# A convolution by transforms: emptying the transform's bank pairs with two engines, and four smaller moves at its start

## The chip, the cores and the metric

The kernel runs on one core of one Trainium2 chip. The core has TensorE for matmuls (PE in the profile, with its weight loads as PEld), VectorE (DVE), ScalarE (ACT), GpSimd (POOL) and SyncE (SP), which here only issues DMAs. Matmul results go to PSUM, eight banks of 512 fp32 values in each of 128 partitions; ScalarE and VectorE read them from there. The metric is the device time in microseconds (us) of one execution; lower is better. A result is the median of several executions.

## The reference

The reference is a convolution over the sequence with three taps, a batch norm and a SiLU. The input x has 2 images of 2048 rows and 1024 channels, w has 3 taps of 1024 x 1024, all in bf16:

```python
xp = jnp.pad(x, ((0, 0), (P, P), (0, 0)))          # P = K // 2 = 1
y = sum(jnp.einsum('bsc,cd->bsd', xp[:, k:k + S, :], w[k]) for k in range(K))
inv_std = 1.0 / jnp.sqrt(var + 1e-5)
y = (y - mean) * (g * inv_std) + b
return _silu(y)
```

## The kernel before

**The algorithm.** Six neighbouring output rows are computed from eight input rows by way of eight points (0, 1, -1, 2, -2, 1/2, -1/2 and infinity, numbered j = 0 to 7). Input and weights are each transformed to the eight points, multiplied there, and the eight products are combined to six outputs. So 342 groups of six rows (342 columns) need 8 products where a direct convolution would need 18.

**Transform of the input.** The rows come in windows of 128 rows, each with 21 groups of six. For an image `bi` and a channel tile `ct` (128 of the 1024 channels), 16 windows lie in one SBUF tile, 512 KB, called x00 to x07 and x10 to x17 below (image, channel tile). A matmul takes a window as its weights and the constant matrix `rm` (8 points x 21 groups, 168 columns) as what is streamed, so a window costs one matmul of 168 columns (line 231). A job (`Jobs.do`) is 6, 6 or 4 windows, three jobs to a tile, 48 in all. Its results lie in a pair of neighbouring PSUM banks, half of the windows in each, and one instruction of ScalarE ("a", line 249) or VectorE ("d", line 251) empties both banks, 1008 or 672 elements a partition, into `T_sb`, as bf16. The few groups left over in each image are the short tile (`load_small`, `do_short`, line 240).

**Transform of the weights.** The output channels come in 8 tiles of 128 (`dc`). For each, the six inner points need u = e +- o, with e one of w0 + w2, w0 + 4 w2, 4 w0 + w2 and o one of w1, 2 w1, 2 w1. Points 0 and infinity use the raw taps w0 and w2. For dc = 0 POOL makes everything (`prepare_first`): e0, 4 w2, e1, 4 w0, e2, 2 w1, then the six u in the order of points 1, 3, 2, 4, 5, 6. POOL then goes on with dc = 1 (`prepare_second`).

**Products.** A unit is one `dc` and one image. For a point it accumulates eight matmuls of 342 columns, one for each channel tile, into a bank (line 279; in the first unit line 398). ScalarE and VectorE combine the banks (line 294), ScalarE applies SiLU (line 298), SP stores. Units alternate between banks 0 to 3 and 4 to 7. The second unit begins with point 1 of image 1, in bank 7, and needs all of image 1's transform.

**The first unit.** `First` (dc 0, image 0) runs among the transform. Its matmuls are a list `todo`: first points 0 and infinity, channel tile by channel tile, into banks 0 and 1, then points 1, 3, 2, 4, 5 and 6. When a point's eight matmuls are out, its bank is copied, by the engine that `COPIES` names.

**What sets the order.** Each engine works through its own queue in the written order; waits between queues are semaphores. The string `ORDER` gives the order of the start: "Aa" is a job into bank pair A, emptied by ScalarE, a number so many matmuls of the first unit, "s2d" the short tile into bank 2, "z5" five matmuls on zeros, "+" a combination of the first unit put off till there. Pair A is banks 4 and 5, B 6 and 7, C 2 and 3, D 0 and 1. SP issues the loads in the written order (lines 522 to 537): image 0's tiles, among them taps 0 and 2 of the first weights, tap 1, image 1's first tile, its short tile in three pieces, its other tiles, the weights of dc = 1. Six x tiles have buffers, so that a load waits for the matmuls of the tile six before it.

Of the kernel before, what the change touches and what calls it, by code (L numbers as in the profile page):

```python
# [9 lines left out]
FP32 = mybir.dt.float32  # L10
BF16 = mybir.dt.bfloat16
ENG = mybir.EngineType

P = 128
R = 6
NJ = 8
WT = 21
XBUFS = 6
LROWS = 48
SROW = 66  # L20
# [6 lines left out]

BANKS = {"A": 4, "B": 6, "C": 2, "D": 0}
ORDER = (
    "Aa Ba Cd Da Ad Ba s2d z5 Da Bd Ca Da Bd Aa Cd Da Aa Bd Da Cd Aa Bd 3 Ca 2 Aa Bd 2 Ca 2 Aa 2 Bd "  # L30
    "Ca 5 Aa Cd Ba 7 s4d Ca Bd 2 Aa 2 Ca 2 Bd Aa 2 Ca 2 Ad Ba 2 Ca 2 Bd Aa 2 Ca 2 + Ad Ba 2 Ca 2 + 2 "
    "Ba 1 Aa"
)
COPIES = {0: "d", 7: "a", 1: "d", 3: "d", 2: "d", 5: "a"}

@with_exitstack
def kernel(
# [9 lines left out]
    nc = tc.nc  # L47
# [30 lines left out]
    nc.scalar.dma_start(out=rm, in_=rm_in)  # L78
    prm = consts.tile([P, 4, DC], BF16, name="prm")

    zeros = consts.tile([P, 256], FP32, name="zeros")
    nc.vector.memset(zeros, 0.0)
    for _ in range(3):
        nc.tensor.matmul(ps[:, 3, 0:256], lhsT=zeros[:, 0:P], rhs=zeros, start=True, stop=True)
    dummy = consts.tile([P, 2], FP32, name="dummy")
    nc.vector.memset(dummy, 0.0)

# [3 lines left out]
    small = xlpool.tile([P, CT * P], BF16, name="xl")  # L91
    nc.vector.memset(small, 0.0)

    def load_small(bi, cuts=()):
        cuts = (0, *cuts, LROWS)
        for lo, hi in zip(cuts, cuts[1:]):
            nc.sync.dma_start(out=small[bi * SROW + lo:bi * SROW + hi], in_=xl[bi, lo:hi])

    def load_x(bi, ct, parts=1, second=nc.scalar):
        t = xpool.tile([P, NF, P], BF16, name="xw")  # L100
        xt[bi, ct] = t
        step = NF // parts
        for q in range(parts):
            s = slice(q * step, (q + 1) * step)
            (second if q else nc.sync).dma_start(out=t[:, s], in_=x[bi, ct, :, s])
# [18 lines left out]
    def scaled(src, by, eng):  # L124
        t = spool.tile([P, CT, P], BF16, name="w1x2")
        if eng is nc.scalar:
            nc.scalar.mul(t, src, by)
        else:
            eng.tensor_scalar(t, src, by, 0.0, op0=ALU.mult, op1=ALU.add)
        return t  # L130

    def double_w(dc, eng):
        double[dc] = scaled(raw[dc][:, 1], 2.0, eng)

    def even(dc, q, a, b):
        sums[dc, q] = epool.tile([P, CT, P], FP32, name=f"e{q}")
        nc.gpsimd.tensor_tensor(sums[dc, q], a, b, op=ALU.add)  # L137
# [7 lines left out]
    def transform_w(dc, q, signs=(0, 1)):  # L145
        o = double[dc] if q else raw[dc][:, 1]
        if (dc, q) not in wts:
            wts[dc, q] = upool.tile([P, 2, CT, P], BF16, name=f"u{q}")
        for i in signs:
            nc.gpsimd.tensor_tensor(wts[dc, q][:, i], sums[dc, q], o, op=(ALU.add, ALU.subtract)[i])  # L150
# [13 lines left out]
        act_work.append(lambda: double_w(dc, nc.scalar))  # L164
        dve_work.extend((second, third))

    def prepare_first(dc):

        w0, w2 = raw[dc][:, 0], raw[dc][:, 2]

        def evens():
            even(dc, 0, w0, w2)
            even(dc, 1, scaled(w2, 4.0, nc.gpsimd), w0)
            even(dc, 2, scaled(w0, 4.0, nc.gpsimd), w2)

        def left():
            double_w(dc, nc.gpsimd)
            for q, i in ((0, 0), (1, 0), (0, 1), (1, 1), (2, 0), (2, 1)):
                transform_w(dc, q, (i,))

        return evens, left

    def prepare_second(dc):
        w0, w2 = raw[dc][:, 0], raw[dc][:, 2]
# [34 lines left out]
    class Jobs:  # L219
# [6 lines left out]
        def do(self, bank, eng):  # L226
            bi, ct, f, nf = self.todo.pop(0)
            per = nf // 2
            src = ps[:, bank:bank + 2, 0:per * NJ * WT].rearrange("p b (f j n) -> p b f j n", f=per, j=NJ)
            for q in range(nf):  # L230
                nc.tensor.matmul(src[:, q // per, q % per], lhsT=xt[bi, ct][:, f + q], rhs=rm, start=True, stop=True)  # L231
            dst = T_sb[bi][:, ct, :, f * WT:(f + nf) * WT].rearrange("p j (b f n) -> p j b f n", b=2, f=per)
            self.out(dst, src.rearrange("p b f j n -> p j b f n"), eng)

        def do_short(self, bank, eng):
            bi = self.short.pop(0)
# [136 lines left out]
    class First(Unit):  # L373
# [3 lines left out]
        def __init__(self, dc, bi):  # L377
            super().__init__(dc, bi, 0)
            self.sd = dpool.tile([P, 4, NB], FP32, name="sd")
            self.t = [  # L380
                consts.tile([P, 2, NB], FP32, name="f0"), ypool2.tile([P, 2, NB], FP32, name="t1"),
                consts.tile([P, 2, NB], FP32, name="f2"),
            ]
            self.kept = consts.tile([P, 2, NB], FP32, name="kept")
            self.todo = [(j, q, False, ct) for ct in range(CT) for j, q in ((0, 0), (NJ - 1, 1))] + [
                (j, q, add, ct) for j, q, add in (
                    (1, 1, False), (3, 0, False), (2, 1, True), (4, 0, True), (5, 2, False), (6, 2, True),
                ) for ct in range(CT)
            ]
            self.p, self.later = {}, []  # L390

        def do(self):
            j, q, add, ct = self.todo.pop(0)
            if j == 0 or j == NJ - 1:
                lhsT = raw[self.dc][:, 0 if j == 0 else 2, ct]
            else:
                lhsT = wts[self.dc, (j - 1) // 2][:, (j - 1) % 2, ct]
            nc.tensor.matmul(  # L398
                self.bank[q], lhsT=lhsT, rhs=T_sb[self.bi][:, ct, j, :],
                start=not add and ct == 0, stop=ct == CT - 1, skip_group_check=True,  # L400
            )
            if ct == CT - 1:
                self.behind(j, q)
# [28 lines left out]

        def finish(self):
            while self.todo:
                self.do()
            b2, b3 = self.bank[2:]
            self.combine(b3, b2, -0.5, self.p[5])
            for t, a in zip(self.t, (-1.6, -0.4, -0.1)):
                self.combine(t, self.high, a, t)
# [91 lines left out]
            load_w(0, (0, 2))  # L531
    load_w(0, (1,))
    load_x(1, 0, 2, nc.sync)
    load_small(1, (15, 41))
    for ct in range(1, CT):
        load_x(1, ct)
    load_w(1, (0, 1, 2))

    evens, left = prepare_first(0)
    evens()
    left()
    second = list(prepare_second(1))
    second.pop(0)()
    jobs, unit = Jobs(), First(0, 0)
    for token in ORDER.split():
        if token == "+":
            unit.later.pop(0)()
        elif token[0] == "z":  # L550
            z = zeros.bitcast(BF16)
            for _ in range(int(token[1:])):
                nc.tensor.matmul(ps[:, 0, 0:192], lhsT=z[:, 0:P], rhs=z[:, 0:192], start=True, stop=True)
        elif token[0] == "s":
            jobs.do_short(int(token[1]), token[2])
        elif token[0] in BANKS:
            jobs.do(BANKS[token[0]], token[1])
        else:
            for _ in range(int(token)):
                unit.do()  # L560
    for f in unit.later:
        f()
    while unit.todo[0][0] != 6:
        unit.do()
    second.pop(0)()
    seq = [(dc, bi) for dc in range(DC) for bi in range(B)]
    prev = unit
# [105 lines left out]
```

## Time and profile before

| | |
|---|---|
| median of 3 runs | 181.75 us (181.49 to 181.86) |
| the profiled execution | 181.6 us, its span 179.8 us |
| TensorE busy | 173.3 us, 96% of the span |
| VectorE, ScalarE, POOL busy | 148.2, 110.8, 140.6 us |
| x00's first transform matmul | 3.95 us |
| x03's first transform matmul | 10.83 us |
| last transform matmul's job begins | 33.55 us |
| second unit's first matmul | 35.01 us |
| one transform matmul in the queue | 0.073 us |
| one product matmul in the queue | 0.145 us |

Times inside the execution are counted from the start of the span. A matmul's own row shows 0.24 or 0.30 us, because matmuls overlap; what one costs TensorE is the distance between the starts of two. A row of a group gives the number of instructions, their busy time, the mean time of one in ns, and the idle time of the engine ahead of them with what ended it.

### The profile page before, as it was taken

To read this page: it belongs to the slowest core of one execution; us is meant where nothing else is said; L and a number is where in the kernel's file an instruction comes from. 1 tells how busy PE (TensorE), PEld (TensorE's weight loads), DVE (VectorE), ACT (ScalarE), POOL (GpSimd) and SP (SyncE) were. 2 spreads that over 40 slices of the span, in tenths; PEclk is the share of its full clock that TensorE was granted. 3 is DMA by queue.
4 is the path that set the end of the run, shared out by engine and by line. 5 is a ranking of instruction groups with operands and counts; after the bars stand their busy time and mean duration, and the time that the engine had idled before them with its cause. 6 is when DMAs were issued, how large, how long until landed. Compare 5 with 4: busy or idle time off the path is not lost.

```text
span 179.8 us, 3491 instructions
## 1 busy us (share of the span) xinstructions
PE 173.3 (96%) x1372; PEld 124.4 (69%) x1372; DVE 148.2 (82%) x193; ACT 110.8 (62%) x175; POOL 140.6 (78%) x77
## 2 busy tenths in 40 slices
PE   7889999999999999999999999999999999999991
PEld 5768888766666666666666666666666666668891
DVE  1568788987969999998898989898998997766792
ACT  3779989968364747365545654555456454573774
POOL 2499999999997979999999999999979978000000
PEclk9999999999999999999999999999999999999999
DMA  5999993170325030823073306430303020213033
GB/s 161 373 415 380 401 417 132 51 303 4 131 79 231 0 131 0 225 86 131 0 177 133 131 0 127 183 131 2 128 7 131 0 112 25 87 44 128 8 142 121
DMA packets 7507, 24.58 MB, mean 137 GB/s; under 512 B 1123, under 2 KB 1635, under 8 KB 7491
## 3 DMA queue, kind: packets, MB, share of 16 engines
q1 hardware_dynamic: 6915, 23.74, 36.1%
q10 hardware_dynamic: 576, 0.63, 1.0%
q8 instruction: 10, 0.16, 0.4%
q14 instruction: 6, 0.05, 0.1%
HBM read 14.93 MB, written 9.44 MB: 136 GB/s over the span
## 4 chain that ended last, share of the span: by engine, by line
PE 88%; DMA 5%; DVE 3%; ACT 1%; issue 0%; ACTq 0%; DVEq 0%
PE ps L279 75%; PE ps L231 8%; DMA xw<-in_x_dram 5%; PE ps L398 5%; DVE ps L294 2%; DVE t L294 1%; ACT yh L298 1%; ACT T_sb L249 1%; ACTq L78 0%; DVEq L662 0%; DVE sd L294 0%; PE ps L240 0%; PE ps L596 0%; DVEq L294 0%
## 5 line engine op out<-in xcount | busy, mean ns | idle before, releaser
L279 PE MATMUL ps<-T_sb,u 128*128 128x342 bf16 (+2 forms) x768 | 109.4, 298 | 0.0
L279 PEld LDWEIGHTS <-u 128*128 128x128 bf16 x768 | 72.2, 97 | 32.8 <-POOL u L150 0.3
L150 POOL TENSOR_TENSOR u<-e,w1x 128x1024 bf16<-128x1024 f32 x32 | 71.5, 2259 | 5.6 <-DVE e L143 5.5
L279 PE MATMUL ps<-T_sb,wch 128*128 128x342 bf16 (+2 forms) x256 | 39.5, 299 | 0.4 <-DVE ps L294 0.4
L294 DVE SCALAR_TENSOR_TENSOR t<-ps,sd 128x684 f32<-128x684 f32 (+2 forms) x49 | 37.6, 819 | 0.6
L298 ACT ACTIVATE yT<-ps,beta,scale 128x342 bf16<-128x342 f32 (+1 forms) x42 | 29.1, 727 | 12.6 <-PE ps L279 12.6
L150 POOL TENSOR_TENSOR u<-e,wch 128x1024 bf16<-128x1024 f32 x16 | 35.7, 2247 | 0.5
L279 PEld LDWEIGHTS <-wch 128*128 128x128 bf16 x256 | 24.2, 97 | 11.1 <-issue 0.5
L288 ACT COPY pc<-ps 128x342 f32<-128x342 f32 (+2 forms) x32 | 13.6, 424 | 28.4 <-PE ps L279 25.7
L249 ACT CAST T_sb<-ps 128x1008 bf16<-128x1008 f32 (+1 forms) x32 | 27.3, 879 | 3.9 <-PE ps L231 3.5
L251 DVE CAST T_sb<-ps 128x1008 bf16<-128x1008 f32 (+2 forms) x18 | 19.3, 1094 | 9.7 <-PE ps L231 9.2
L294 DVE SCALAR_TENSOR_TENSOR ps<-ps,t 128x684 f32<-128x684 f32 (+2 forms) x32 | 26.5, 829 | 0.7
L294 DVE SCALAR_TENSOR_TENSOR ps<-ps,pc 128x342 f32<-128x342 f32 (+2 forms) x34 | 16.9, 497 | 12.1 <-PE ps L279 8.8
L231 PE MATMUL ps<-rm,xw 128*128 128x168 bf16 x256 | 23.4, 239 | 1.6 <-DMA xw<-in_x_dram 1.4
L143 DVE SCALAR_TENSOR_TENSOR e<-wch 128x1024 f32<-128x1024 bf16 x12 | 24.6, 2052 | 0.0
L231 PEld LDWEIGHTS <-xw 128*128 128x128 bf16 x256 | 19.9, 99 | 4.8 <-DMA xw<-in_x_dram 2.4
L137 POOL TENSOR_TENSOR e<-wch 128x1024 f32<-128x1024 bf16 x8 | 19.0, 2372 | 0.1
L298 ACT ACTIVATE yT<-t,beta,scale 128x684 bf16<-128x684 f32 x15 | 14.4, 958 | 0.0
L294 DVE SCALAR_TENSOR_TENSOR t<-ps,t 128x684 f32<-128x684 f32 (+2 forms) x17 | 13.9, 817 | 0.0
L288 ACT COPY sd<-ps 128x342 f32<-128x342 f32 (+2 forms) x16 | 6.8, 426 | 10.3 <-PE ps L279 9.3
L290 ACT ACTIVATE pc<-ps 128x342 f32<-128x342 f32 (+2 forms) x16 | 7.0, 438 | 8.8 <-PE ps L279 6.1
L294 DVE SCALAR_TENSOR_TENSOR sd<-pc,ps 128x342 f32<-128x342 f32 (+2 forms) x17 | 8.2, 484 | 4.1 <-ACT sd L288 4.0
(45 smaller groups left out, 67.3 us busy)
## 6 DMA issues: line engine op xcount, KB each, us to landing
out_dram<-yT SPq DMA_DIRECT2D x15, 576.0 KB, 2.8
xw<-in_x_dram SPq DMA_DIRECT2D x13, 512.0 KB, 6.4
wch<-in_w_dram SPq DMA_DIRECT2D x7, 768.0 KB, 5.5
xw<-in_x_dram SPq DMA_DIRECT2D x4, 256.0 KB, 8.4
wch<-in_w_dram SPq DMA_DIRECT2D x3, 256.0 KB, 5.2
xw<-in_x_dram ACTq DMA_DIRECT2D x2, 256.0 KB, 4.6
out_dram<-yh SPq DMA_DIRECT2D x1, 256.0 KB, 2.0
out_dram<-yh SPq DMA_DIRECT2D x1, 128.0 KB
```

Of the source, the lines that this page charges most:

```text
L137: nc.gpsimd.tensor_tensor(sums[dc, q], a, b, op=ALU.add)
L143: nc.vector.scalar_tensor_tensor(out=e, in0=f, scalar=4.0, in1=h, op0=ALU.mult, op1=ALU.add)
L150: nc.gpsimd.tensor_tensor(wts[dc, q][:, i], sums[dc, q], o, op=(ALU.add, ALU.subtract)[i])
L231: nc.tensor.matmul(src[:, q // per, q % per], lhsT=xt[bi, ct][:, f + q], rhs=rm, start=True, stop=True)
L249: nc.scalar.copy(dst, src)
L251: nc.vector.tensor_copy(dst, src)
L279: nc.tensor.matmul(self.bank[q], lhsT=lhsT, rhs=T_sb[self.bi][:, ct, j, nsl], start=not add and ct == 0, stop=ct == CT - 1, skip_group_che ...
L288: nc.scalar.copy(dst, self.bank[q])
L290: nc.scalar.mul(dst, self.bank[q], by)
L294: nc.vector.scalar_tensor_tensor(out=out, in0=in0, scalar=scalar, in1=in1, op0=ALU.mult, op1=op1)
L298: nc.scalar.activation(self.yT[:, rows, self.y0:self.y0 + self.hi - self.lo], src, ACT.Silu, bias=beta[:, dc:dc + 1], scale=scale[:, dc:dc ...
L398: nc.tensor.matmul(self.bank[q], lhsT=lhsT, rhs=T_sb[self.bi][:, ct, j, :], start=not add and ct == 0, stop=ct == CT - 1, skip_group_check ...
```

## The change

Five things change, all in the first 40 us.

- **Halves.** A job's letters may now be two: "Dda" empties pair D with VectorE on the first bank and ScalarE on the second, each with an instruction of its own of half the size. One letter still empties both banks with one instruction.
- **Points 0 and infinity** of the first unit go to banks 2 and 3 (pair C) instead of 0 and 1, and have a list of their own, `ends`; a plain number takes from it, "p" and a number from the other list. Six of them stand ahead of x03's first job; before, the first three stood behind x06's second job. Their two copies are VectorE's; the copies of points 2 and 3 ScalarE's (`COPIES`).
- **Two weight multiples.** "m1a" and "m2a" let ScalarE compute 4 w0 and 2 w1; POOL keeps 4 w2. The class `FirstWeights` issues POOL's steps in the old order, each as soon as its multiple has been issued.
- **Loads.** The short tile of image 1 is one load, behind all of image 1's tiles.
- **Warm-up and the rest.** Two fp32 matmuls of 416 columns on zeros instead of three of 256 (each is two passes); the five "z" matmuls go. Image 0's short tile lies in bank 6 and is emptied by ScalarE; image 1's stands near the end of the order instead of in the middle. `ORDER` is written anew. Its last numbers leave one matmul of point 4 and the eight of point 5 for behind the string, the combinations put off being issued between these.

```diff
@@ -27,11 +27,11 @@
 BANKS = {"A": 4, "B": 6, "C": 2, "D": 0}
 ORDER = (
-    "Aa Ba Cd Da Ad Ba s2d z5 Da Bd Ca Da Bd Aa Cd Da Aa Bd Da Cd Aa Bd 3 Ca 2 Aa Bd 2 Ca 2 Aa 2 Bd "
-    "Ca 5 Aa Cd Ba 7 s4d Ca Bd 2 Aa 2 Ca 2 Bd Aa 2 Ca 2 Ad Ba 2 Ca 2 Bd Aa 2 Ca 2 + Ad Ba 2 Ca 2 + 2 "
-    "Ba 1 Aa"
+    "Dda Bad Dda Cad Aad s6a Dda Cda Ada Dda 5 m1a 1 Bad Aad Da Bda Ada 2 Bda Dad Aad 1 Ba Dda 1 Ada 1 "
+    "Bd 1 Dda Ada Bda 1 m2a 1 Dad Ada Ba 2 p7 Ada Cad Ba p1 Aad p3 Cad p1 Ba p1 Ada Cad p3 Bad p1 Ada p1 "
+    "Cda p1 Ba p6 + Ada + p2 Cad p1 Bad Aad p2 s2a Bda p1 Ada + Cad Ba Aa"
 )
-COPIES = {0: "d", 7: "a", 1: "d", 3: "d", 2: "d", 5: "a"}
+COPIES = {0: "d", 7: "d", 1: "d", 3: "a", 2: "a", 5: "a"}
 @with_exitstack
 def tile_standalone__batchnorm__prompt_kernel(
@@ -78,10 +78,10 @@
     nc.scalar.dma_start(out=rm, in_=rm_in)
     prm = consts.tile([P, 4, DC], BF16, name="prm")
-    zeros = consts.tile([P, 256], FP32, name="zeros")
+    zeros = consts.tile([P, 416], FP32, name="zeros")
     nc.vector.memset(zeros, 0.0)
-    for _ in range(3):
-        nc.tensor.matmul(ps[:, 3, 0:256], lhsT=zeros[:, 0:P], rhs=zeros, start=True, stop=True)
+    for _ in range(2):
+        nc.tensor.matmul(ps[:, 3, 0:416], lhsT=zeros[:, 0:P], rhs=zeros, start=True, stop=True)
...
@@ -91,10 +91,8 @@
     small = xlpool.tile([P, CT * P], BF16, name="xl")
     nc.vector.memset(small, 0.0)
-    def load_small(bi, cuts=()):
-        cuts = (0, *cuts, LROWS)
-        for lo, hi in zip(cuts, cuts[1:]):
-            nc.sync.dma_start(out=small[bi * SROW + lo:bi * SROW + hi], in_=xl[bi, lo:hi])
+    def load_small(bi):
+        nc.sync.dma_start(out=small[bi * SROW:bi * SROW + LROWS], in_=xl[bi])
     def load_x(bi, ct, parts=1, second=nc.scalar):
         t = xpool.tile([P, NF, P], BF16, name="xw")
@@ -164,21 +162,34 @@
         act_work.append(lambda: double_w(dc, nc.scalar))
         dve_work.extend((second, third))
-    def prepare_first(dc):
-
-        w0, w2 = raw[dc][:, 0], raw[dc][:, 2]
-
-        def evens():
-            even(dc, 0, w0, w2)
-            even(dc, 1, scaled(w2, 4.0, nc.gpsimd), w0)
-            even(dc, 2, scaled(w0, 4.0, nc.gpsimd), w2)
-
-        def left():
-            double_w(dc, nc.gpsimd)
-            for q, i in ((0, 0), (1, 0), (0, 1), (1, 1), (2, 0), (2, 1)):
-                transform_w(dc, q, (i,))
-
-        return evens, left
+    class FirstWeights:
+
+
+
+        def __init__(self, dc):
+            w0, w2 = raw[dc][:, 0], raw[dc][:, 2]
+            self.dc, self.src, self.made = dc, ((w2, 4.0), (w0, 4.0), (raw[dc][:, 1], 2.0)), {}
+            elsewhere = [int(t[1]) for t in ORDER.split() if t[0] == "m"]
+            self.steps = [(None, lambda: even(dc, 0, w0, w2))]
+            self.steps += [(i, lambda i=i: self.multiple(i, nc.gpsimd)) for i in (0,) if i not in elsewhere]
+            self.steps += [(0, lambda: even(dc, 1, self.made[0], w0))]
+            self.steps += [(i, lambda i=i: self.multiple(i, nc.gpsimd)) for i in (1,) if i not in elsewhere]
+            self.steps += [(1, lambda: even(dc, 2, self.made[1], w2))]
+            self.steps += [(i, lambda i=i: self.multiple(i, nc.gpsimd)) for i in (2,) if i not in elsewhere]
+            self.steps += [
+                (2 if q else None, lambda q=q, i=i: transform_w(dc, q, (i,)))
+                for q, i in ((0, 0), (1, 0), (0, 1), (1, 1), (2, 0), (2, 1))
+            ]
+            self.own = [i for i in range(3) if i not in elsewhere]
+
+        def multiple(self, i, eng):
+            self.made[i] = t = scaled(*self.src[i], eng)
+            if i == 2:
+                double[self.dc] = t
+
+        def go(self):
+            while self.steps and (self.steps[0][0] in self.made or self.steps[0][0] in (None, *self.own)):
+                self.steps.pop(0)[1]()
     def prepare_second(dc):
         w0, w2 = raw[dc][:, 0], raw[dc][:, 2]
@@ -230,7 +241,12 @@
             for q in range(nf):
                 nc.tensor.matmul(src[:, q // per, q % per], lhsT=xt[bi, ct][:, f + q], rhs=rm, start=True, stop=True)
             dst = T_sb[bi][:, ct, :, f * WT:(f + nf) * WT].rearrange("p j (b f n) -> p j b f n", b=2, f=per)
-            self.out(dst, src.rearrange("p b f j n -> p j b f n"), eng)
+            src = src.rearrange("p b f j n -> p j b f n")
+            if len(eng) == 1:
+                self.out(dst, src, eng)
+            else:
+                for b in range(2):
+                    self.out(dst[:, :, b], src[:, :, b], eng[b])
         def do_short(self, bank, eng):
             bi = self.short.pop(0)
@@ -382,15 +398,16 @@
                 consts.tile([P, 2, NB], FP32, name="f2"),
             ]
             self.kept = consts.tile([P, 2, NB], FP32, name="kept")
-            self.todo = [(j, q, False, ct) for ct in range(CT) for j, q in ((0, 0), (NJ - 1, 1))] + [
+            self.ends = [(j, q, False, ct) for ct in range(CT) for j, q in ((0, 2), (NJ - 1, 3))]
+            self.todo = [
                 (j, q, add, ct) for j, q, add in (
                     (1, 1, False), (3, 0, False), (2, 1, True), (4, 0, True), (5, 2, False), (6, 2, True),
                 ) for ct in range(CT)
             ]
             self.p, self.later = {}, []
-        def do(self):
-            j, q, add, ct = self.todo.pop(0)
+        def do(self, todo):
+            j, q, add, ct = todo.pop(0)
             if j == 0 or j == NJ - 1:
                 lhsT = raw[self.dc][:, 0 if j == 0 else 2, ct]
             else:
@@ -432,7 +449,7 @@
         def finish(self):
             while self.todo:
-                self.do()
+                self.do(self.todo)
             b2, b3 = self.bank[2:]
             self.combine(b3, b2, -0.5, self.p[5])
             for t, a in zip(self.t, (-1.6, -0.4, -0.1)):
@@ -531,37 +548,38 @@
             load_w(0, (0, 2))
     load_w(0, (1,))
     load_x(1, 0, 2, nc.sync)
-    load_small(1, (15, 41))
     for ct in range(1, CT):
         load_x(1, ct)
+    load_small(1)
     load_w(1, (0, 1, 2))
-    evens, left = prepare_first(0)
-    evens()
-    left()
-    second = list(prepare_second(1))
-    second.pop(0)()
+    first_w = FirstWeights(0)
+    first_w.go()
     jobs, unit = Jobs(), First(0, 0)
     for token in ORDER.split():
         if token == "+":
             unit.later.pop(0)()
-        elif token[0] == "z":
-            z = zeros.bitcast(BF16)
-            for _ in range(int(token[1:])):
-                nc.tensor.matmul(ps[:, 0, 0:192], lhsT=z[:, 0:P], rhs=z[:, 0:192], start=True, stop=True)
+        elif token[0] == "m":
+            first_w.multiple(int(token[1]), {"a": nc.scalar, "d": nc.vector}[token[2]])
+            first_w.go()
         elif token[0] == "s":
             jobs.do_short(int(token[1]), token[2])
         elif token[0] in BANKS:
-            jobs.do(BANKS[token[0]], token[1])
+            jobs.do(BANKS[token[0]], token[1:])
         else:
-            for _ in range(int(token)):
-                unit.do()
+            todo = unit.todo if token[0] == "p" else unit.ends
+            for _ in range(int(token.lstrip("p"))):
+                unit.do(todo)
+    while unit.todo[0][0] == 4:
+        unit.do(unit.todo)
     for f in unit.later:
         f()
-    while unit.todo[0][0] != 6:
-        unit.do()
+    while unit.todo[0][0] == 5:
+        unit.do(unit.todo)
+    second = list(prepare_second(1))
+    second.pop(0)()
     second.pop(0)()
     seq = [(dc, bi) for dc in range(DC) for bi in range(B)]
     prev = unit
```

## The prediction

> **What bounds the kernel now.** I read the engine totals first, then the stretches of the start, the chain that ended last, the groups by shape and the order of instructions.
>
> ```profile
> PE 173.3 (96%) x1372; PEld 124.4 (69%) x1372; DVE 148.2 (82%) x193; ACT 110.8 (62%) x175; POOL 140.6 (78%) x77
> ```
>
> TensorE bounds the span, so the change can only pay through TensorE's idle time or its matmul count. The count of useful matmuls is unchanged. Where is the idle time?
>
> ```profile
> 8.00:10.00 2.00, 1.82 (x25) 1.62 (x21) 1.41 (x3) 1.53 (x3) 1.60 (x6) 1.00 1.06 424
> 10.00:12.00 2.00, 1.17 (x16) 1.13 (x16) 1.07 (x2) 1.41 (x3) 1.93 (x2) 1.00 1.03 416
> 12.00:14.00 2.00, 2.00 (x25) 1.66 (x23) 2.00 (x2) 1.91 (x3) 1.92 (x2) 1.00 1.03 412
> ```
> ```profile
> 1.16 4.56 DMA xw<-in_x_dram
> ...
> 5.74 5.05 DMA xw<-in_x_dram
> ...
> 10.83 2.33 PE ps L231 x28
> ...
> 13.19 1.01 ACT T_sb L249
> ...
> 16.51 0.29 PE ps L231 x4
> 16.80 0.29 PE ps L398 x2
> ...
> 37.50 126.70 PE ps L279 x872
> ```
>
> Stretches: the columns after the length are busy time of PE, PEld, DVE, ACT and POOL, then granted clock and DMA. The chain gives start, length, what. A transform matmul takes 0.29/4 = 0.073 us of TensorE's time, a product matmul 126.70/872 = 0.145 us. Tile x03 (image 0, channel tile 3; x10 is image 1, tile 0) lands at 10.79, and TensorE waits for it although DMA is full (416 GB/s). From 8.63 to 14.24 TensorE does 54 transform matmuls, 54 x 0.073 = 3.9 us of 5.6: **1.7 us are idle**, 1.0 of them before x03, the rest waits for banks and for the next tile. From 14.24 to 34.9 there is none: 170 transform matmuls, 56 products and the short ones make 12.4 + 8.1 + 0.2 = 20.7 us. Later only 0.15 us are lost, at 48.95, to a weight sum of POOL. So the change can win 1.9 us at most, and what it loads on the engines that empty the banks counts from 11 to 35 us.
>
> ```profile
> L249 ACT CAST T_sb<-ps 128x1008 bf16<-128x1008 f32 x18 | 17.8, 1000 | 3.7 <-PE ps L231 3.5
> L251 DVE CAST T_sb<-ps 128x1008 bf16<-128x1008 f32 x14 | 16.7, 1205 | 4.5 <-PE ps L231 4.3
> L249 ACT CAST T_sb<-ps 128x672 bf16<-128x672 f32 x14 | 10.1, 724 | 0.2
> L251 DVE CAST T_sb<-ps 128x672 bf16<-128x672 f32 x2 | 1.7, 853 | 4.9 <-PE ps L231 4.9
> ```
> ```profile
> 9.26 1.62 ACT L249 CAST T_sb<-ps 128x1008 bf16<-128x1008 f32 x2 [0.47 <-PE ps L231]
> ...
> 34.57 0.87 DVE L294 SCALAR_TENSOR_TENSOR f<-ps,sd 128x684 f32<-128x684 f32 x1
> 35.36 0.86 DVE L294 SCALAR_TENSOR_TENSOR t<-ps,sd 128x684 f32<-128x684 f32 x1
> ```
>
> Read two things here. The cost of a cast against its size (mean ns), and its spacing: two ScalarE casts of 1.00 and 0.73 us fill 1.62 us, so a waiting one starts 0.105 us before its predecessor ends; on VectorE 0.87 us is followed after 0.79, 0.08 earlier.
>
> **The change, part by part.**
>
> *Halves.* From the four rows: ScalarE 0.17 us + 0.82 ns an element, VectorE 0.15 us + 1.05 ns (the 384-element cast at 552 ns fits). A half of 504 elements takes 0.59 us on ScalarE, 0.68 on VectorE; one of 336 takes 0.45 and 0.50. A pair is empty about 0.6 us after its matmuls, not 1.0 to 1.2, but both engines pay a start each. From x03 to the last tile there are 39 jobs: 25 large and 5 small in halves, 1 large and 7 small on ScalarE alone, 1 small on VectorE. ScalarE: 25 x 0.59 + 5 x 0.45 + 1.0 + 7 x 0.72 = 23.0, and the short tile 0.5, two multiples 2.1, the copies of points 2 and 3 0.9: 26.5 us in 43 instructions. VectorE: 25 x 0.68 + 5 x 0.50 + 0.85 = 20.3, seven copies and combinations of one bank at 0.50 3.5: 23.8 in 38. TensorE: 21.3. By durations ScalarE would bound this stage; by spacing it needs 26.5 - 43 x 0.105 = 22.0, VectorE 23.8 - 38 x 0.08 = 20.8. (Before: ScalarE 23.1, VectorE 19.4 by durations.)
>
> *Waits between halves.* A half reads one bank; I take it that it waits for that bank's matmuls alone, and the next job's first matmuls for the first bank alone, as the units already read one bank while another is written. If both wait for the whole pair, see the second rival. A cast that waits on two engines starts some 0.06 us later (before: up to 28.17 after the matmul's 28.10); nothing to 0.3 us in all, and I take 0, as most casts queue behind another.
>
> *Points 0 and infinity.* 6 of their 16 matmuls move ahead of x03's job: 6 x 0.145 = 0.87 us into the hole. They need the weights of taps 0 and 2 (landed 8.9 and 9.5), x00 to x02 emptied, and banks 2 and 3 free.
>
> *Multiples.* Two of POOL's three, 1.05 us each there, go to ScalarE's queue (1.06 us each, by its multiples of output tile 1), one behind x02's casts (10.22 to 11.27, while x03's matmuls run), one behind x07's. POOL's first u then ends at 19.4 instead of 21.5, the sixth at 30.4 instead of 31.9, so that the 0.15 us at 48.95 go (if not, the sum is 0.15 less). The second u waits 0.3 us for the second multiple (19.7) and ends at 21.9, 0.8 us ahead of its use at 22.7. Behind a multiple on ScalarE's queue stand the casts of x03 and x10: the first still find it free when their matmuls end, x10's start 0.8 us late, and TensorE reaches their banks only 2 us later.
>
> *DMA.* The second short tile goes from three issues ahead of image 1's second tile to one behind all of image 1. Before, SP holds these issues from 10.84 to 14.68, each behind an older landing; image 1's tile 1 is now issued at some 12.1. DMA is full, so only the short tile's 96 KB no longer lie ahead, 0.23 us at 416 GB/s: it lands 0 to 0.2 us before the 20.7 of before and is used at 20.9 below; taken 0. The short tile lands by 30 and is used at 30.5, weights of output tile 1 follow it.
>
> *Warm-up.* Six passes at 0.43 us become four of 416/256 x 0.43 = 0.69: TensorE is free at 4.1, not 3.9. x00's second half lands at 5.72 and hides it. The five z matmuls (0.4 us at 8.2) go: x02 starts at 8.27. The granted clock is 1.0 from 5.44 on in this trace; were it late, some 16 matmuls at 0.07 us more would lie ahead of x02's landing at 8.25 or in the hole: 0 to 0.5, taken 0 since the warm-up keeps TensorE busy as long.
>
> **The sum.** I walked the written order with these rules: matmuls 0.073 and 0.145; a cast starts 0.2 us after its bank's last matmul, or 0.105 (0.08) before its predecessor ends; a bank is written 0.055 us after its cast ends. On the old order from x03 on they give cast starts 11.47, 11.91, 12.37, 13.03, as in the trace. In the new order x02's casts end at 10.32 and 10.58. Four products run from 9.63 to 10.21, two wait for x02 and run from 10.64 to 10.93. x03 starts at 10.93 (before 10.83) with 0.87 us done ahead. Then x05 starts at 13.77, x07 at 16.67, x10 at 18.34. Up to here TensorE idles 0.55 us in some eight short waits for banks, and VectorE's queue lags up to 0.8 us. Point 1's seven matmuls end at 20.94; image 1's tile 1 follows at once. From there no waits: last transform matmul 32.80, points 4 and 5 to 34.11. The last two casts end at 33.71 and 34.32, in time for the second unit, which **starts at 34.11 instead of 35.01: -0.90**, and -0.15 at 48.95 makes **-1.05 us**. Behind that TensorE runs through to its last product; nothing there is changed. The profiled execution took 181.6 us (span 179.8), 0.15 under the median 181.75; 181.6 - 1.05 = 180.55, and 0.15 for the median: **180.7 us**. Its own range: no idle at all, 0.55 more, 180.1; 0.6 us of extra waits, 181.3.
>
> **A rule that speaks against it.** The Trainium skill, VectorE: DVE Perf Modes, section The DRAIN you can't avoid, says that the next VectorE instruction cannot issue before the pipe is empty, and to keep the number of instructions low. The rows above disagree (0.79 us apart for one of 0.87), though none is a half of a cast; by the rule the time would be the third rival's.
>
> **The rivals.**
> 1. *The halves wait for whole pairs.* Casts then start up to 0.22 us later and banks free as much later: the walk by pairs has the second unit at 35.31, +0.30 - 0.15 = +0.15, 181.9. For: a job now signals once, at its last matmul. Against: that cast reads both banks.
> 2. *The early products do not fit* (weights or x02 late, x03 pushed back as far): the 0.87 is lost, 181.6.
> 3. *VectorE's queue becomes the bound* (the other side). If a VectorE instruction started only at its predecessor's end, x02's last half ends at 11.17, x03 starts 0.6 late, and by image 1's tile 1 the lag is 1.6 us: unit two at 35.7, +0.55, 182.3. With ScalarE without overlap too, the walk gives 37.5, +2.4, 184.2. It decides, in proportion, from 0.08 x 0.9/1.6 = 0.045 us more for each VectorE instruction. For: up to 0.8 us of lag already. Against: the spacing rows.
>
> **How the numbers follow.** Forecast 0.58, pairs 0.18, no early products 0.09, VectorE or both without overlap 0.15. A change of 0.2%, 0.36 us, is about what can be told from none: bounds 181.39 and 182.11. Faster: the forecast and 0.02 of the pairs, 0.60. Same: 0.10 of pairs, 0.06 of no early products, 0.16. Slower: the rest, 0.24. Range 180.0 to 182.4: down to no idle, up to the pairs and VectorE's lag; the full load of 184.2 is left out.
>
> **What would show it.** Right: products of L398 with raw weights before 10.8; ScalarE and VectorE casts of 504 elements at 0.59 and 0.68 us, starting before predecessors end; PE full from 20 us; the second unit near 34.1. Wrong: halves well over 0.68 us, or TensorE idle again and again for VectorE's casts from 11 to 20 us; x03's matmuls far behind 10.9; ScalarE's last cast behind 35 us; POOL's sums late at 48 us.

## The result, and the profile after

The changed kernel took 181.21 us (median of 11, 181.11 to 181.66) against 181.79 (181.49 to 182.17) for the kernel before on the same chip. The medians are 0.58 us apart; the ratio, which goes by means, is 0.9973 with a 95% interval of 0.9963 to 0.9983, some 0.5 us faster. The forecast was 1.05 us faster, 180.7. The direction was right and the size about half.

The profiled execution of after took 181.66 us, 0.45 above its own median, since one tile landed late in it; two more profiles of the same kernel (runs e1 and e11 below, 181.36 and 181.23 us) are read beside it. Its engine totals, and the stretches of the start (columns after the length: PE, PEld, DVE, ACT, POOL, granted clock, DMA share, GB/s):

```profile
PE 173.9 (97%) x1365; PEld 123.2 (69%) x1365; DVE 152.2 (85%) x214; ACT 111.0 (62%) x195; POOL 137.4 (76%) x75
```
```profile
10.00:12.00 2.00, 1.74 (x19) 1.14 (x18) 0.94 (x3) 1.64 (x4) 1.93 (x2) 1.00 1.04 424
12.00:14.00 2.00, 2.00 (x25) 1.66 (x23) 2.00 (x4) 2.00 (x5) 1.92 (x2) 1.00 1.02 418
14.00:21.00 7.00, 6.70 (x77) 5.51 (x75) 6.79 (x13) 6.67 (x14) 5.79 (x4) 1.00 1.03 413
21.00:30.00 9.00, 9.00 (x103) 7.85 (x101) 7.65 (x15) 8.14 (x17) 9.00 (x5) 1.00 0.81 314
30.00:35.00 5.00, 4.92 (x58) 4.08 (x56) 4.96 (x11) 4.63 (x9) 4.92 (x3) 1.00 0.07 14
```

From 10 to 12 us TensorE is now busy 1.74 of 2.00 us, 1.17 before: most of the hole is filled. VectorE and ScalarE have 41 instructions more between them and are full from 12 to 14 us, and nearly so up to 21. The order of TensorE's instructions shows what fills the hole (start, length, engine, line; L415 are products, L242 transform matmuls):

```profile
9.65 0.74 PE L415 MATMUL ps<-T_sb,wch 128*128 128x342 bf16 x4
10.65 0.46 PE L415 MATMUL ps<-T_sb,wch 128*128 128x342 bf16 x2 [0.26 <-DVE T_sb L267]
11.01 1.19 PE L242 MATMUL ps<-rm,xw 128*128 128x168 bf16 x14
```

Four products run at 9.65, two wait for x02's cast and run at 10.65, and x03 follows at 11.01. The forecast had 9.63, 10.64 and 10.93.

The chain that ended last (start, length, what) says where the rest stayed:

```profile
9.54 9.25 DMA xw<-in_x_dram
18.79 0.05 issue
18.84 1.40 PE ps L242 x16
...
28.06 0.72 ACT T_sb L265
28.78 0.42 ACT sd L424
29.21 0.02 issue
29.23 0.51 DVE sd L310
29.75 0.59 DVE T_sb L267
30.34 0.41 DVE sd L310
30.75 0.30 DVE T_sb L267
31.05 0.21 issue
31.26 0.51 DVE T_sb L267
31.77 0.04 issue
31.81 0.38 PE ps L242 x3
...
37.51 126.54 PE ps L295 x872
```

Before, this chain ran from 13 to 34 us almost wholly over TensorE. Now it leaves TensorE twice. At 18.79 TensorE waits for image 1's first tile; that is the late tile of this one execution. From 28.06 to 31.81 the chain runs over ScalarE's casts, ScalarE's copy of point 2 (L424), VectorE's put-off combinations (L310) and VectorE's casts (L267), and only then back to TensorE. This detour stands in every trace of the changed kernel.

The stage in numbers, all us. "Waits" is TensorE's idle time; x03, x11 and unit 2 stand for their first matmul (x11 is image 1's tile 1).

| | x03 | unit 2 | x03 to unit 2 | waits x03 to x11 | waits x11 to unit 2 |
|---|---|---|---|---|---|
| before | 10.83 | 35.01 | 24.18 | 0.71 | 0 |
| forecast | 10.93 | 34.11 | 23.18 | 0.55 | 0 |
| after, first trace | 11.01 | 35.02 | 24.01 | 0.98 | 0.43 |
| after, e1 | 11.10 | 34.72 | 23.62 | 0.58 | 0.44 |
| after, e11 | 10.97 | 34.58 | 23.61 | 0.58 | 0.44 |

### The profile page after: what moved, and what is told of

The parts are those of the page before. It is cut to its first block, busy times and chain, and to the rows that moved or that the text cites. A ratio compares the mean times of both kernels' runs of the same rounds, so it can differ in the third digit from the quotient of the medians.

```text
span 179.8 us, 3538 instructions
## 1 busy us (share of the span) xinstructions
PE 173.9 (97%) x1365; PEld 123.2 (69%) x1365; DVE 152.2 (85%) x214; ACT 111.0 (62%) x195; POOL 137.4 (76%) x75
## 4 chain that ended last, share of the span: by engine, by line
PE 87%; DMA 5%; DVE 4%; ACT 1%; issue 1%; DVEq 0%
PE ps L295 75%; PE ps L242 7%; DMA xw<-in_x_dram 5%; PE ps L415 3%; PE ps L84 2%; DVE ps L310 2%; DVE t L310 1%; DVE T_sb L267 1%; DVE sd L310 1%; ACT yh L314 1%; ACT T_sb L265 0%; ACT sd L424 0%; DVE zeros L82 0%; DVEq L680 0%; PE ps L256 0%
## 5 line engine op out<-in xcount | busy, mean ns | idle before, releaser
L148 POOL TENSOR_TENSOR u<-e,w1x 128x1024 bf16<-128x1024 f32 x32 | 69.4, 2192 | 7.8 <-DVE e L141 7.6
L310 DVE SCALAR_TENSOR_TENSOR t<-ps,sd 128x684 f32<-128x684 f32 (+2 forms) x49 | 37.6, 819 | 0.6
L148 POOL TENSOR_TENSOR u<-e,wch 128x1024 bf16<-128x1024 f32 x16 | 36.5, 2300 | 1.8 <-DMA wch<-in_w_dram 1.2
L267 DVE CAST T_sb<-ps 128x504 bf16<-128x504 f32 (+2 forms) x40 | 23.4, 644 | 5.4 <-PE ps L242 5.2
L265 ACT CAST T_sb<-ps 128x504 bf16<-128x504 f32 (+4 forms) x49 | 25.4, 597 | 3.8 <-PE ps L242 3.5
L310 DVE SCALAR_TENSOR_TENSOR ps<-ps,t 128x684 f32<-128x684 f32 (+2 forms) x32 | 26.5, 829 | 0.7
L310 DVE SCALAR_TENSOR_TENSOR ps<-ps,pc 128x342 f32<-128x342 f32 (+2 forms) x34 | 16.9, 496 | 10.1 <-PE ps L295 7.2
L141 DVE SCALAR_TENSOR_TENSOR e<-wch 128x1024 f32<-128x1024 bf16 x12 | 25.4, 2116 | 0.0
L242 PE MATMUL ps<-rm,xw 128*128 128x168 bf16 x256 | 23.8, 240 | 0.4 <-DMA xw<-in_x_dram 0.3
L242 PEld LDWEIGHTS <-xw 128*128 128x128 bf16 x256 | 20.0, 99 | 4.5 <-DMA xw<-in_x_dram 2.2
L310 DVE SCALAR_TENSOR_TENSOR t<-ps,t 128x684 f32<-128x684 f32 (+2 forms) x17 | 13.9, 817 | 0.0
L310 DVE SCALAR_TENSOR_TENSOR sd<-pc,ps 128x342 f32<-128x342 f32 (+2 forms) x17 | 8.2, 482 | 5.2 <-ACT sd L304 5.2
```

The costliest lines, as they stand in the source:

```text
L141: nc.vector.scalar_tensor_tensor(out=e, in0=f, scalar=4.0, in1=h, op0=ALU.mult, op1=ALU.add)
L265: nc.scalar.copy(dst, src)
L267: nc.vector.tensor_copy(dst, src)
L310: nc.vector.scalar_tensor_tensor(out=out, in0=in0, scalar=scalar, in1=in1, op0=ALU.mult, op1=op1)
```

## The experiments

Unless it is said otherwise an edit is made to the changed kernel. Ratios are to the kernel before, run beside it on the same chip, with 95% intervals; the kernel before had medians of 181.88 (e1 to e4), 182.07 (e5 to e8), 181.85 (e9 to e11) and 181.78 us (e12).

**e1, the changed kernel again.**

> The changed kernel once more, for a second trace of it and its time against the kernel before on this chip. The profiled execution of the first had x10 land at 18.8 us (forecast 18.3) and took 181.66, 0.45 above the median of its runs. Theory B (the late landing of x10 takes what was missing): this trace has it again, TensorE idle for some 0.4 us from 18.4, in a typical execution. If the landing was that execution's own, the idle time is gone here, the second unit begins near 34.5 and the span is near 179.3. Either way some 0.3 to 0.7 us below the kernel before.

Measured: 181.27 us (181.09 to 181.41), 0.9964 [0.9952, 0.9977]. The first trace's long wait at x10 is gone, the waits up to x11 are 0.58 us, but the 0.44 us behind x11 are there. VectorE's row of instructions in this trace:

```profile
28.92 0.51 DVE L310 SCALAR_TENSOR_TENSOR sd<-ps,kept 128x342 f32<-128x342 f32 x1 [1.05 <-ACT sd L424]
29.35 0.68 DVE L267 CAST T_sb<-ps 128x504 bf16<-128x504 f32 x1
29.94 0.50 DVE L310 SCALAR_TENSOR_TENSOR sd<-pc,ps 128x342 f32<-128x342 f32 x1
30.36 2.27 DVE L267 CAST T_sb<-ps 128x504 bf16<-128x504 f32 x4
```

VectorE stands idle for 1.05 us until ScalarE's copy of point 2 is through (in this trace 28.43 to 28.89; the combination starts 0.03 us later). Half of this is not the copy's: VectorE's last cast ends at 27.87, point 2's last matmul at 28.39, and the copy starts 0.04 us after that matmul, so that ScalarE's casts ahead of it do not hold it up. Before, VectorE was still in a cast when point 2's last matmul ended (30.96), and then made the copy and the combination with no idle time between:

```profile
31.03 0.50 DVE L409 TENSOR_SCALAR sd<-ps 128x342 f32<-128x342 f32 x1
31.45 0.50 DVE L294 SCALAR_TENSOR_TENSOR sd<-ps,kept 128x342 f32<-128x342 f32 x1
```

In e1 the casts of x15 and x16 behind the first combination, with a second one between them, come late, and TensorE waits 0.11, 0.27 and 0.08 us for their banks, at 30.1, 31.5 and 32.1.

**e2, the copy of point 2 on VectorE.**

```diff
-COPIES = {0: "d", 7: "d", 1: "d", 3: "a", 2: "a", 5: "a"}
+COPIES = {0: "d", 7: "d", 1: "d", 3: "a", 2: "d", 5: "a"}
```

> One letter: the copy of point 2 is VectorE's again, as in the kernel before, all else is the changed kernel. Theory A (VectorE's first put-off combination reads the bank that ScalarE copies, waits for that copy, which stands behind ScalarE's cast of x14, and VectorE's casts of x15 and x16 come late): no wait of VectorE at 28.2 to 29.2 us, TensorE's idle time from 30.9 to 31.8 gone, second unit 0.3 to 0.4 us earlier, time 0.3 to 0.4 us below the changed kernel's. Theories B and C (VectorE's queue is the bound in itself): no gain, or 0.1 to 0.4 slower, since VectorE gets 0.42 us more to do.

Measured: 181.15 us (180.98 to 181.22), 0.9958 [0.9946, 0.9969]; 0.12 us below e1, waits behind x11 0.37 us. VectorE's instructions:

```profile
28.20 0.52 DVE L426 TENSOR_SCALAR sd<-ps 128x342 f32<-128x342 f32 x1 [0.56 <-PE ps L415]
28.63 0.50 DVE L310 SCALAR_TENSOR_TENSOR sd<-ps,kept 128x342 f32<-128x342 f32 x1
29.05 0.68 DVE L267 CAST T_sb<-ps 128x504 bf16<-128x504 f32 x1
```

The wait for the other engine is gone, but VectorE still stands idle for 0.56 us until point 2's products are through, and its own copy then takes 0.43 us of its queue. It gets to the cast 0.88 us after point 2's last matmul has ended (28.17), in e1 0.96 us after it: only 0.08 us earlier. (The cast stands at 29.05 for 29.35, but this whole trace is some 0.22 us ahead of e1's at point 2.) So the theory that the wait for ScalarE alone costs the 0.44 us fell. What is in the way is the whole row ahead of the casts: the wait for point 2, the copy (or the wait for it) and two combinations.

**e3, without x10's landing.** The jobs of image 1's first tile read x07's tile instead; the output is not the reference's.

```diff
-                nc.tensor.matmul(..., lhsT=xt[bi, ct][:, f + q], ...)
+                nc.tensor.matmul(..., lhsT=xt[(0, 7) if (bi, ct) == (1, 0) else (bi, ct)][:, f + q], ...)
```

> The three jobs of x10 transform tile x07's rows in place of x10's own (so image 1's channel tile 0 is computed from the wrong rows); x10 is still loaded, so that the transfers are as many, but nothing waits for its landing. Theory B: TensorE's wait near 18.4 to 18.8 us goes, second unit 0.3 to 0.5 us earlier, time 0.3 to 0.5 below the changed kernel's. Theory A: at most 0.1 us, as VectorE's wait at 28 us decides, or the two add up and this alone gives part.

Measured: 181.23 us (181.09 to 181.45), 0.9966 [0.9953, 0.998], as e1. The landing of x10 costs the median nothing that can be seen; the 0.4 us of the first trace are that execution's.

**e4, the two multiples back on POOL.**

```diff
-    "... Dda 5 m1a 1 Bad ... Bda 1 m2a 1 Dad ..."
+    "... Dda 5 1 Bad ... Bda 1 1 Dad ..."
```

> The two weight multiples are POOL's again, all else is the changed kernel. ScalarE has 2.1 us less to do, POOL's first u ends 2.1 us later, near 22.4, while the changed kernel uses it at 20.4. If the multiples earn their place, TensorE idles some 1.5 to 2 us before point 1 and the time is 0.5 to 1.5 us above the changed kernel's. If ScalarE's queue were the bound of the stage, taking 2.1 us from it would give 0.5 us or more back and the two would nearly cancel.

Measured: 183.06 us (182.72 to 183.32), 1.0063 [1.0048, 1.0077]. The waits of TensorE in that trace (engine, line, what for: us in total, times, longest; the first row is the weight load's of the same matmul):

```profile
PEld L415 <- POOL u L148: 1.5, 1, 1.5
PE ps L415 <- POOL u L148: 1.2, 1, 1.2
```

Without the multiples on ScalarE, point 1 waits for POOL's first u, 1.31 us of TensorE at 21.8 (x03 to unit 2: 24.94 against 23.62). By the medians the two multiples are worth 1.8 us in this order. Of the 0.5 us beyond that wait, the trace shows x03 beginning 0.36 us later than in e1; whether that belongs to the edit is open.

**e5, the put-off combinations behind the last halves.**

```diff
-    "Cda p1 Ba p6 + Ada + p2 Cad p1 Bad Aad p2 s2a Bda p1 Ada + Cad Ba Aa"
+    "Cda p1 Ba p6 Ada p2 Cad p1 Bad Aad p2 s2a Bda p1 Ada Cad + + + Ba Aa"
```

> The three put-off combinations stand behind the job of x17's first windows instead of among x15 to x16; ScalarE still copies point 2. Taking that copy from ScalarE gave only some 0.1 us, because VectorE then copied itself (0.43 us) ahead of the same combination. Theory A, mended: what makes TensorE wait 0.46 us from 30 to 32 us is VectorE standing behind a copy of point 2, whoever makes it, and two combinations, 1.0 us in a row. With them behind the last halves the wait goes: second unit 0.35 to 0.45 us earlier, time 0.3 to 0.5 us below the changed kernel's. Theory C (VectorE has too much to do there in all): the wait stays or comes back at x17 or behind it, no gain.

Measured: 181.00 us (180.79 to 181.1), 0.9933 [0.991, 0.9956]. The waits behind x11 fall from 0.44 to 0.16 us, and the second unit starts at 34.43, 0.29 us earlier than in e1, a little less than expected. VectorE now waits for TensorE in this place, not for ScalarE:

```profile
28.77 0.69 DVE L267 CAST T_sb<-ps 128x504 bf16<-128x504 f32 x1 [0.92 <-PE ps L242]
```

It stands idle nearly as long as in e1 (0.92 us), but at its end comes the cast of x15, at 28.77 instead of 29.35, with x11 at the same time in both traces (21.11 and 21.12). What costs is not VectorE's idle time but the late cast.

**e6, points 0 and infinity later.** The six early products stand where the next ones of their list stood; all else is unchanged.

```diff
-    "... Dda 5 m1a 1 Bad ... Bd 1 Dda Ada Bda 1 m2a 1 Dad Ada Ba 2 p7 ..."
+    "... Dda m1a Bad ... Bd 3 Dda Ada Bda 3 m2a 1 Dad Ada Ba 4 p7 ..."
```

> The six products of points 0 and infinity ahead of x03 stand behind x06 and x07 and x10 (two, two and two more there); all else is the changed kernel. By the forecast they are worth 0.87 us where they are, of which later waits for banks can give back up to 0.5 here: 0.4 to 0.9 us above the changed kernel's time, x03's first matmul some 0.1 to 0.2 us earlier. Rival (they push x03 back as far as they save): no change within 0.2 us.

Measured: 181.65 us (181.34 to 184.27), 0.9979 [0.9956, 1.0002]; x03 to unit 2 takes 24.13 us, 0.51 more than in e1. The stretches:

```profile
10.00:12.00 2.00, 1.03 (x15) 1.03 (x16) 1.02 (x3) 2.00 (x5) 1.95 (x1) 1.00 1.03 420
...
14.00:21.00 7.00, 7.00 (x82) 6.10 (x80) 6.83 (x13) 6.37 (x14) 6.36 (x4) 1.00 1.04 416
```

The hole is back (1.03 of 2.00 us), but from 14 to 21 us TensorE has no idle time left. The 0.87 us moved into the hole bring 0.51, since 0.35 us come back as waits for banks (0.58 us up to x11 with them, 0.23 without).

**e7, no halves.** Each job's two letters are replaced by the one letter that the same job had before.

```diff
-    "Dda Bad Dda Cad Aad s6a ..."
+    "Da Ba Dd Ca Ad s6a ..."
```

> Each job is emptied by one instruction of the engine that emptied the same job in the kernel before; banks, products, multiples, loads are the changed kernel's. By the forecast a pair is then taken for 1.0 to 1.2 us, not 0.6, and ScalarE, which has the multiples as well, waits less often for its share: TensorE waits again and again for banks from 11 to 21 us, 0.5 to 2 us above the changed kernel's time. If the halves are not what pays, within 0.2 us of it, or faster, since the two engines have some 5 us less to do.

Measured: 185.76 us (185.52 to 186.04), 1.0193 [1.0167, 1.0219]: by the two ratios some 4.2 us slower than the changed kernel (0.9964 in e1), where no more than 2 had been thought of. Two of the places, in TensorE's order:

```profile
13.19 1.24 PE L240 MATMUL ps<-rm,xw 128*128 128x168 bf16 x12 [0.36 <-ACT T_sb L263]
...
15.15 1.32 PE L240 MATMUL ps<-rm,xw 128*128 128x168 bf16 x16 [0.43 <-DVE T_sb L265]
```

TensorE waits for whole casts again and again, 3.55 us up to x11 and 1.81 behind it. The new order takes pair D for three of the first six jobs and keeps pair C for the products soon after; it counts on pairs that come free in about half the time.

**e9, halves alone, on the kernel before.** All 48 jobs of the old order in halves, nothing else of the change.

```diff
-    "Aa Ba Cd Da Ad Ba s2d z5 ..."
+    "Aad Bad Cda Dad Ada Bad s2d z5 ..."
```

> The kernel before with halves alone: each of the 48 jobs is emptied by both engines, ScalarE on the first bank where the job was ScalarE's, else on the second; order, banks, products, multiples and loads are those of before. From x03 on VectorE then has 26 x 0.68 + 13 x 0.50 and 4.0 of short tile, copies and combinations: 28.2 us by durations in 47 instructions, 24.3 by spacing, where the stage has 23.5. By the forecast's rule of spacing: 0.5 to 2 us slower than the kernel before. If VectorE started an instruction only at its predecessor's end: 4 us or more slower. If halves pay whatever stands around them: faster.

Measured: 183.12 us (182.58 to 184.03), 1.0063 [1.004, 1.0086], 1.27 us slower than before. Its VectorE from 11 us on (this profile is the slowest of its runs):

```profile
11.16 3.28 DVE L251 CAST T_sb<-ps 128x504 bf16<-128x504 f32 x6 [0.44 <-PE ps L229]
```

Each job now takes of both engines a start each, and this order still has VectorE copy points 2 and 3: TensorE waits 1.34 us up to x11, 0.71 before, and 1.0 behind it, 0 before. In this trace x03 also begins 0.86 us later than before (11.69 for 10.83); how much of that is due to the halves is open. So halves for all 48 jobs are no gain in the old order; halves for some of them only were not tried. With e7 the parts can't be told apart by adding: the gain belongs to halves and order together.

**e8 and e10, e5 and one job more.** The second of the two edits has ScalarE empty x06's last job.

```diff
-    "Bd 1 Dda Ada Bda 1 m2a ..."
-    "Cda p1 Ba p6 + Ada + p2 Cad p1 Bad Aad p2 s2a Bda p1 Ada + Cad Ba Aa"
+    "Ba 1 Dda Ada Bda 1 m2a ..."
+    "Cda p1 Ba p6 Ada p2 Cad p1 Bad Aad p2 s2a Bda p1 Ada Cad + + + Ba Aa"
```

> The combinations late as in the other kernel of this set, and the last job of x06 emptied by ScalarE instead of VectorE. By the forecast's walk VectorE's queue lags 0.8 us there and TensorE waits 0.2 and 0.15 us for its banks at x07 and x10; ScalarE has 0.4 us idle before x07. So 0.2 to 0.35 us below the kernel with the combinations late alone, second unit near 34.1. If ScalarE's multiple behind x07 is then late, or the wait moves to ScalarE, no gain.

> The kernel with the combinations late and x06's last job on ScalarE once more, beside the changed kernel on the same chip: 0.4 to 0.8 us below the changed kernel's median and 1.0 to 1.4 below the kernel before, second unit near 34.1. If the gain of the earlier set was the chip's, within 0.2 us of the changed kernel.

Measured: 180.55 us (180.4 to 181.19), 0.9915 [0.989, 0.994], and again 180.49 us (180.36 to 180.7), 0.992 [0.9897, 0.9942]. This version beats both kernels. The last stretch and VectorE's row in it, of e10:

```profile
30.00:35.00 5.00, 5.00 (x57) 4.02 (x55) 4.86 (x11) 4.85 (x9) 4.92 (x4) 1.00 0.25 69
```
```profile
29.32 3.32 DVE L267 CAST T_sb<-ps 128x504 bf16<-128x504 f32 x6 [0.33 <-PE ps L242]
32.56 0.50 DVE L310 SCALAR_TENSOR_TENSOR sd<-ps,kept 128x342 f32<-128x342 f32 x1
```

Six casts run one behind the other, the combinations follow at 32.56, when no job is waiting for VectorE any more, and TensorE is busy 5.00 of 5.00 us. From x03 to unit 2 it takes 23.07 us in e8 and 23.17 in e10. The forecast had 23.18 for the changed kernel, and it takes these two edits to get there. The last 0.16 us of waits behind x11, left in e5, are gone with the second edit; how a job of x06 does that was not followed up.

**e11, the changed kernel a third time.**

> The changed kernel a third time, for the comparison on one chip: 0.4 to 0.7 us below the kernel before; TensorE idle 0.4 to 0.45 us between image 1's tile 1 and the second unit, 0.5 to 1.0 between x03 and there, the more where x10 lands late.

Measured: 181.39 us (181.14 to 181.63), 0.9964 [0.9947, 0.9981], with the waits of e1, 0.58 and 0.44 us.

**e12, the copy of point 2 into another tile.** ScalarE's copy and VectorE's combination read one PSUM bank, but they also write parts of one SBUF tile, `sd`; either could be what the combination waits for. Here the copy goes to t2's tile, and the later combinations read other parts of `sd` for it, so that the output is not the reference's.

```diff
-                self.out_of(j, q, sd[:, 0])
+                self.out_of(j, q, self.t[2][:, 0])
-            ... (sd[:, 1:3], sd[:, 0:3:2], sd[:, 0:4:3])
+            ... (sd[:, 1:3], sd[:, 1:4:2], sd[:, 2:4])
```

> The changed kernel, but ScalarE's copy of point 2 is written to another tile than the one that the put-off combinations write (the tile t2 is given, and the three f combinations read other columns of sd in its place, so the output is not the reference's). It tells what VectorE's first put-off combination waits for. If it is the bank that both read, the combination still starts within 0.05 us of the copy's end, VectorE's idle time ahead of it stays near 1.0 us, TensorE's idle time from image 1's tile 1 to the second unit stays at 0.4 to 0.45 us, and the time is that of the changed kernel, 0.3 to 0.7 us under the kernel before. If it is the common tile sd, the combination starts some 0.7 us ahead of the copy's end, VectorE is idle for under 0.4 us there, TensorE's idle time falls below 0.2 us and the time by 0.2 to 0.3 us more.

Measured: 181.28 us (181.07 to 181.52), 0.9966 [0.9954, 0.9979], waits behind x11 0.43 us. ScalarE's copy, then VectorE's combination:

```profile
28.43 0.46 ACT L424 ACTIVATE f<-ps 128x342 f32<-128x342 f32 x1
```
```profile
28.92 0.52 DVE L310 SCALAR_TENSOR_TENSOR sd<-ps,kept 128x342 f32<-128x342 f32 x1 [1.05 <-ACT f L424]
```

The copy writes `f` now and the combination waits for it all the same, to 28.92. All that the two still share is the bank that both read.

## Why the prediction was right in direction and half in size

**The step that failed** is "From there no waits", of the stretch from x11 to the second unit. The walk counted the combinations as 0.50 us of VectorE's queue each, and none of its written rules says what a combination has to wait for. In the new order the first put-off combination stands right behind the products that end point 2 ("p6 +"). There VectorE is idle for 1.05 us (e1): 0.52 us until point 2's last matmul has ended, and 0.53 until ScalarE has copied point 2 out of the bank that the combination reads too. Then two combinations lie ahead of casts that TensorE needs, and the first of these casts starts at 29.35 where it could have started at 28.77 (e5). That makes 0.43 to 0.44 us of TensorE in every trace of this order, also in e3, e4, e6 and e12, where other things were changed. e12 shows that the combination waits for the copy when only the bank is common. e2 shows that which engine makes the copy matters little: 0.37 us of the waits remain. e5 shows that the place of the combinations is what costs: behind the casts they leave 0.16 us. In e8 and e10, with one more job moved to ScalarE, nothing is left, and the stage takes what was forecast.

The Trainium skill, PSUM — Partial Sum Buffer, section PSUM bank collisions raise a hardware error, says that accesses of two engines to one bank in the same partitions have to be kept apart in time, two reads too. The trace agrees as to the order: the combination starts 0.03 us behind the copy's end (e1) and stays there when nothing but the bank is common (e12). What would happen to two reads at once no run here shows.

**The sum, mended.** The forecast -1.05, and 0.44 for these waits, 0.11 for x03 at 11.04 instead of 10.93 (mean of the first trace, e1, e11 and e12), 0.03 for waits of 0.58 instead of 0.55 up to x11: -0.47 us. Measured: -0.58, -0.61, -0.46 and -0.50 us by the medians. The 0.11 is within the scatter: over the nine traces that share this start (the first, e1 to e3, e5, e8, e10 to e12) x03 begins at 10.63 to 11.10, at 10.95 in the mean, and with that the sum is -0.56.

**What held:**

- *Halves.* Forecast 0.59 us on ScalarE and 0.68 on VectorE; the groups by shape of the first trace (count | busy us, mean ns | idle ahead) say 0.596 and 0.676:

```profile
L267 DVE CAST T_sb<-ps 128x504 bf16<-128x504 f32 x31 | 19.7, 676 | 5.3 <-PE ps L242 5.2
L265 ACT CAST T_sb<-ps 128x504 bf16<-128x504 f32 x31 | 17.1, 596 | 3.6 <-PE ps L242 3.5
```

- *Each half waits for its own bank* (against the first rival). x03's first matmul starts at 11.01; its first half starts 0.43 us later on ScalarE and its second 0.65 later on VectorE, that is three matmuls of 0.073 us and 0.2, and six and 0.2:

```profile
11.44 5.63 ACT L265 CAST T_sb<-ps 128x504 bf16<-128x504 f32 x11 [0.36 <-PE ps L242]
```
```profile
11.66 7.72 DVE L267 CAST T_sb<-ps 128x504 bf16<-128x504 f32 x13 [1.06 <-PE ps L242]
```

- *The early products fit* (against the second rival): they are out by 11.0 us, and x03 is pushed back by some 0.1 us only (11.10 in e1, 10.97 in e6). Without them there (e6) the stage from x03 to the second unit is 0.51 us longer, not the rival's 0.87, since waits for banks go in return.
- *VectorE's spacing* (against the third). Casts of 0.68, 0.50, 0.68 and 0.68 us, 2.54 in sum, fill 2.27 us in e1's row at 30.36: each starts 0.09 us before its predecessor ends. The Trainium skill's rule of the pipe that has to be empty first, weighed in the prediction, would have made these 2.54 if the pipe is taken to be empty at the end of a row. The same section of the Trainium skill, VectorE: DVE Perf Modes, The DRAIN you can't avoid, adds that an instruction that is not held starts earlier, and here the trace agrees with that.
- *Waits up to x11.* Forecast 0.55 us, measured 0.58 twice.
- *POOL.* The first u ends at 19.56 us in e1 (forecast 19.4), the second waits 0.35 for its multiple (0.3), the sixth ends at 30.40 (30.4). From the second unit to the one matmul on zeros ahead of the last unit (line 614) it takes 128.87 us in e1, 129.03 before: the 0.15 us at 48.95 are gone, as counted.
- *Loads and warm-up at nothing*: x02 starts at 8.08 to 8.55 us in the four traces of this order (8.63 before, 8.27 forecast), x10 at 18.37 to 18.51 but for the first trace (18.34 forecast).

## What to carry to other kernels

Ask of each instruction in an engine's queue what it waits for, and what stands behind it. A combination that stands right behind the products it needs waits for the last of them, and here also for the other engine's copy of the same PSUM bank; what counts is that the casts behind it then come late. Work that is not urgent belongs behind the casts for which TensorE waits. Here moving three combinations by a few places, and one cast to the other engine, brought 0.9 us by the medians on top of the change's 0.5 (e10 against e11). The traces show 0.44 of it between x03 and the second unit; 0.34 lies ahead of x03, where the two orders are the same. Halves of a drain and the order that uses them are one change: either one alone, as tried here, made this kernel slower (e7, e9).

## What the runs showed of the hardware that was not expected

The traces point to an instruction fetch that holds up one sixteenth of a load. In every trace the instruction queue moves one packet of 16 KB at 15.6 to 16.8 us, in the middle of the loads; in the first trace of after at 15.84 us, and its record takes 0.97 us. That trace from 15 to 20 us:

```profile
q1 hardware_dynamic: 756, 2.06, 103.4%
q8 instruction: 1, 0.02, 1.2%
```

(Packets, MB, share of 16 engines.) A load lands in sixteen parts. The last part of x10's first half landed at 18.79 us, the last of the other fifteen at 16.84; before it was 18.33 against 17.19, in e1 18.22 against 17.33, in e11 17.98 against 16.89. In e7, where the fetch came at 16.83, the first half was not held up (17.22 against 17.17), the second was (18.83 against 17.86). A tile is there when its last part is, so such a part decides when x10 can begin. But the fetch is in every trace and does not by itself explain the late tile of the first: there one part was 0.45 us behind already at x07, ahead of the fetch (15.99 against 15.54; 15.60 against 15.52 in e11). Why is open; the late tile cost that execution about 0.4 us. No run takes the fetch away, and e3 shows that the landing costs the median nothing here.
